# Pooled attention, mixture of experts and a cosine FFN on one core: a written-out order of steps for each attention unit in place of one order for all

## The chip, the cores and the metric

One core of a Trainium2 chip runs the whole program in one launch. The metric is the device time of an execution in microseconds; the time before is the median of three runs. The profile comes from one further execution, taken by the hardware profiler. PE is TensorE, DVE VectorE, ACT ScalarE, POOL GpSimd and SP SyncE; each engine works off its own queue in order.

## The reference

The output of the attention is the input of the mixture of experts (MoE), and its output that of the last FFN. Cut to what is computed:

```python
# attention: q, k, v (8, 8, 576, 64)
k_p = k.reshape(B, H, Sp, pool, D).mean(axis=3)      # pool = 8, Sp = 72
v_p = v.reshape(B, H, Sp, pool, D).mean(axis=3)
scores = scale * np.matmul(q, k_p.transpose(0, 1, 3, 2))
attn = softmax(scores)
x = np.matmul(attn, v_p)                             # as (4608, 512)
# MoE: 8 experts, the 2 best by noisy logits, w1 (8, 512, 1024), w2 (8, 1024, 512)
noisy_logits = x @ w_gate + np.log1p(np.exp(x @ w_noise)) * noise
out[mask] += top2_w[mask, k, None] * (np.maximum(x[mask] @ w1[e], 0.0) @ w2[e])
# last FFN, d_ff = 2048
h = x @ w_in
return (h * np.cos(h)) @ w_out
```

## The kernel before, in words

**Stages.** The program runs three stages after one another: attention with the gating of the MoE and the scatter of its rows (0 to about 335 us of the profiled execution), the experts, and the last FFN. The change touches the code of the first stage alone.

**Pairs and units.** The eight batches are worked in four pairs (`g` = 0 to 3). A pair has nine row blocks of 64 positions of both batches, 128 rows; two row blocks make a unit, and the fifth unit of a pair has one. That makes 20 units (`UNITS`), numbered 0 to 19; units 4, 9, 14 and 19 are the small ones.

**Steps of a unit.** The loop over `u` (line 747 on) issues the steps of several units interleaved: 
- `S0` to `S3` are `scores(u+2)`: matmuls of q with the pooled K (L432) and DVE's maximum (L434);
- `E0` to `E3` are `expo(u+2)`: ACT's exponentials (L447);
- `N` is `soft_sum(u+1)`: DVE's sum and reciprocal (L457 to L461), and then the multiply of the exponentials by it (L462), on POOL for all units but the last;
- `T0` to `T2` are `e_tr(u)`: PE transposes of the exponentials (L479 to L483) into a PSUM buffer `tr`, of which there are two, and ACT's copy out of it (L485);
- `A0` to `A3` are `av(u)`: matmuls with V (L513), ACT's copy to `xr` (L516), DVE's remainder (L517) and logits (L520, L522);
- `Q0`, `Q1` are `q_tr(u+3)`: transposes of q (L416) and ACT's copy (L417);
- `G` issues steps of the fill list.

Only the order of issue is chosen here: every engine takes its instructions in the order in which the loop issues them, and waits where an operand or a buffer isn't ready.

**The fill list.** It holds work that isn't of the running unit, as a list of functions. For the next pair (`setup_steps`): five steps that pool K (by DVE, or for pairs 2 and 3 by `folded`, with matmuls by the identity, L298), five that pool V, four transposes of K (L313, ACT L320), `scale_v`, four transposes of V (L313), two steps of the projection of the gate's weights (`g_proj1`, `g_proj2`, L372 and L384). For the pair before (`late`): the gating in ten steps (`gating`, L526 on; g1 to g6 below, with `g1` from L546 on, `g3` L559 to L562, `g4a` and `g4b` L569 to L577, `g5` the matmuls of L583 to L588, `g5b` the indices `idx` at L605) and nine `scatter` steps. One `scatter` (L634) has two indirect DMAs (L639) that POOL issues, each behind a one-element memset (L638). In pairs 2 and 3 the list also holds the preparation of the first expert's weights (`prep_steps`): for each weight four `amax` reductions on DVE (L153), of which the last ends with the copy `mbc` (L108), a `scl` step that begins with a PE transpose of `mbc` (L114), and eight steps that split the weights (ACT L171 and DVE L178). In units 18 and 19 it holds four `up` steps (`early_up`, twelve matmuls each, L662) and four `lo` steps.

**What sets the order before.** One string is used for all units (line 738):

```python
ORDER = "S0 G T0 G T1 S1 E0 T2 N A0 G A1 E1 S2 G A2 Q0 E2 G S3 G A3 Q1 G E3".split()
```

At each of its seven `G`, `go` issues the next steps of the list, their number so chosen that the list is spread evenly over what is left of the pair. At a pair border two lists are merged evenly by `mix`.

Of the kernel before, what the change touches and what calls it, by code (L numbers as in the profile page):

```python
# [12 lines left out]
AF = mybir.ActivationFunctionType  # L13
# [12 lines left out]
T0 = [E * 1024 + 128 * i + sum(EXTRA[:i]) for i in range(E)]  # L26
# [11 lines left out]
def tile_attn_moe_ffn(ctx: ExitStack, tc: tile.TileContext, q, k, v, wgate, wnoise, noise,  # L38
                      w1, w2, win, wout, out):
    nc = tc.nc  # L40
    V, A, PL, PE, SP = nc.vector, nc.scalar, nc.gpsimd, nc.tensor, nc.sync

    def dap(src, offset, dims):
        return bass.AP(tensor=src.tensor, offset=src.offset + offset, ap=dims)
# [22 lines left out]
    idf = const.tile([128, 128], F32, name="idf")  # L67
    V.tensor_scalar(idf, jp, 0.0, None, op0=OP.is_equal)

    QT, KT, VT = {}, {}, {}  # L70

    def nop():
        pass

    def load_kv(g, which):
        src, dst = ((k, KT), (v, VT))[which]
        t = ow.tile([128, 5, 2, 512], F32, name="w1", bufs=2)
        for c in range(5):
# [186 lines left out]
    def setup_steps(g):  # L265

        X = {}
        kbd = KBDB[g % 2]

        def pooled(src, nm, i):  # L270
            def f():
                if i == 0:
                    X[nm + "f"] = src.pop(g).rearrange("p c b e -> p (c b) e")
                    n0, n1 = (0, 1280) if nm == "ks" else (1280, 1920)
                    X[nm] = SW[:, n0:n1].rearrange("p (c s d) -> p c s d", c=10, d=D)
                t, o = X[nm + "f"], X[nm]
                n = 64 if nm == "ks" and i == 4 else 128
                t, o = t[0:n, 2 * i:2 * i + 2, :], o[0:n, 2 * i:2 * i + 2, :, :]
                for w in (256, 128):
                    V.tensor_add(t[:, :, 0:w], t[:, :, 0:w], t[:, :, w:2 * w])  # L280
                dup = [n, 2, 2 if nm == "ks" else 1, D]
                V.tensor_add(o, t[:, :, None, 0:D].to_broadcast(dup), t[:, :, None, D:2 * D].to_broadcast(dup))
            return f

        def folded(src, nm, i):

            def f():
                if i == 0:
                    X[nm + "f"] = src.pop(g).rearrange("p c b e -> p (c b) e")
                    n0, n1 = (0, 1280) if nm == "ks" else (1280, 1920)  # L290
                    X[nm] = SW[:, n0:n1].rearrange("p (c s d) -> p c s d", c=10, d=D)
                if i in (0, 4):
                    X["pf"] = pq.tile([128, 512], F32, name="sc", bufs=3)
                t = X["pf"]
                c0, c1, js = (0, 8, range(2 * i, 2 * i + 2)) if i < 4 else (8, 10, range(8))
                n = 64 if nm == "ks" and i == 4 else 128
                for j in js:
                    PE.matmul(t[0:n, 0:64 * (c1 - c0)].rearrange("p (c d) -> p c d", d=D), idf[0:n, 0:n],  # L298
                              X[nm + "f"][0:n, c0:c1, 64 * j:64 * j + 64], start=(j == 0), stop=(j == 7))
                if js[-1] == 7:  # L300
                    k_ = 2 if nm == "ks" else 1
                    A.activation(X[nm][0:n, c0:c1], t[0:n, 0:64 * (c1 - c0)].rearrange("p (c d) -> p c d", d=D)[:, :, None, :]
                                 .to_broadcast([n, c1 - c0, k_, D]), AF.Copy)
            return f

        def tr_half(src, b, half):
# [84 lines left out]

        bh = [(b, h) for b in range(2) for h in range(2)]
        pk, pv = ([pooled(src, nm, i) for i in range(5)] for src, nm in ((KT, "ks"), (VT, "vp")))
        if g in (2, 3):
            pk = [folded(KT, "ks", i) for i in range(5)]
        if g in ():
            pv = [folded(VT, "vp", i) for i in range(5)]
        kt, vt = ([f(*x) for x in bh] for f in (k_tr, v_tr))
        return pk, kt, pv, [scale_v, nop, scale_v2] + vt + [g_proj1, nop, g_proj2]

# [5 lines left out]
    def q_tr(u, half):  # L406
        if u >= NU:
            return
        g, r, n = UNITS[u]
        qt = QT[g]  # L410
        if half == 0:
            QTS[u] = ap_.tile([128, 8, 128], F32, name="qs", bufs=2)
        qs, h0 = QTS[u], 4 * half
        tr = pq.tile([128, 512], F32, name="tr", bufs=2)
        for h in range(4):
            PE.transpose(tr[0:64 * n, 128 * h:128 * h + 128], qt[:, h0 + h, 64 * r:64 * (r + n)], idf)  # L416
        A.activation(qs[0:64 * n, h0:h0 + 4, :], tr[0:64 * n].rearrange("p (h t) -> p h t", h=4), AF.Copy)  # L417
# [316 lines left out]
    fill, late = [], []  # L734

    CUTS = {3: (0, 6), 4: (6, 8)}
    left = [0]
    ORDER = "S0 G T0 G T1 S1 E0 T2 N A0 G A1 E1 S2 G A2 Q0 E2 G S3 G A3 Q1 G E3".split()

    def go():  # L740
        k_ = -(-len(fill) // left[0])
        left[0] = max(left[0] - 1, 1)
        for f in fill[:k_]:
            f()
        del fill[:k_]

    for u in range(NU):
        g, r, n = UNITS[u]
        it = u % 5
        if it == 0:  # L750
            a = []
            if g + 1 < G:
                pk, kt_, pv, sv = setup_steps(g + 1)
                a = pk + pv[:2]
                for i in range(4):
                    a += kt_[i:i + 1] + pv[i + 2:i + 3]
                a += sv
                if g + 2 < G:
                    a.append(lambda g=g: (load_kv(g + 2, 0), load_kv(g + 2, 1)))
            if g == G - 1:  # L760
                a = p2
            fill += mix(a, late)
            late = []
        if g == G - 2 and it == 2:
            p1, p2 = prep_steps(0, "w1"), prep_steps(0, "w2")
            p1.pop(0)()
            p2.pop(0)()
        if g == G - 2 and it == 3:
            fill = mix(fill, p1)
        if g == G - 1 and it in CUTS:  # L770
            r0, r1 = CUTS[it]
            gt = gating(g, r0, r1)
            gt.pop(0)()
            fill += with_ups(gt, (0, 1) if it == 3 else (2, 3)) + [scatter(g, r_) for r_ in range(r0, r1)]
        left[0] = ORDER.count("G") * ((5 if g < G - 1 or it > 2 else 3) - it)
        if g == G - 1 and it == 3:
            left[0] = 6
        for op in ORDER:
            k_ = int(op[1:] or 0)
            if op == "A0":  # L780

                while first_v:
                    first_v.pop(0)()
            if op[0] == "G":
                go()
            elif op[0] == "S":
                scores(u + 2, k_)
            elif op[0] == "E":
                expo(u + 2, k_)
            elif op[0] == "N":  # L790
                soft_sum(u + 1)
            elif op[0] == "T":
                e_tr(u, k_)
            elif op[0] == "A":
                av(u, k_ // 2, k_ % 2)
            else:
                q_tr(u + 3, k_)
# [86 lines left out]
    with tc.For_i(0, nov, 1) as i:  # L884
# [496 lines left out]
    o = work.index((mm2, JOBS.index((E - 1, 0)), 3))  # L1381
# [80 lines left out]
    for c in range(NCF):  # L1462
        plan = prepare(c + 1, lambda: g[:, 14:16, :])
        for q_ in range(4):
# [4 lines left out]
            g = GQ[c, q_] = wp.tile([128, 16, 512], F16, name="ht", bufs=2)  # L1469
# [82 lines left out]
```

## Time and profile before

| | us |
|---|---|
| median of 3 runs | 1796.01 |
| lowest, highest | 1793.70, 1797.31 |
| profiled execution, whole | 1813.74 |
| its span | 1811.6 |
| PE busy in the span | 1733.1 (96%) |
| DVE, ACT, POOL busy | 1052.0, 923.9, 425.0 |
| mean granted clock of PE | 0.976 |
| PE idle after 335 us | 11.45 of 1476.00 |

The page gives the busy time of each engine and the span in 40 slices; the view by stretches gives the same for any piece of the span, with PE's granted clock in it (1.00 is full speed). A timeline lists one engine's instructions in order, with the idle time before each and what ended it in brackets: `[1.35 <-ACT et L485]` is 1.35 us of waiting that ACT's write of `et` at line 485 ended. Neighbouring instructions of one form stand in one row with their count (x3).

### The profile page before, as it was taken

The page shows a single profiled execution, that of the slowest core. Times are in us where ns is not written, and L with a number is a line of the kernel's source. Part 1 is how long each engine was busy: PE and PEld are TensorE (multiplying, and loading weights), DVE is VectorE, ACT ScalarE, POOL GpSimd, SP SyncE. Part 2 cuts the span into 40 slices and gives each one's busy share as a digit, 9 for nine tenths or more (in the row PEclk, how much of TensorE's full clock was granted, in tenths as well). Part 3 has the DMA queues.
Part 4 walks back from the last instruction along what each step waited for, and adds up shares of the span by engine and source line. Part 5 has one row for each costly group of instructions (what it writes and reads, how often), then busy time and mean ns, then how long its engine had stood idle before and what let it go on. Part 6 is the DMA issues. An engine that isn't in the chain of part 4 may idle for free.

```text
span 1811.6 us, 28368 instructions
## 1 busy us (share of the span) xinstructions
PE 1733.1 (96%) x11105; PEld 1014.1 (56%) x11105; DVE 1052.0 (58%) x2010; ACT 923.9 (51%) x1836; POOL 425.0 (23%) x459
## 2 busy tenths in 40 slices
PE   5999787899999999999999998999999999999999
PEld 3665553355444644454545545666666666666665
DVE  7675674464567376435766135665656566565633
ACT  4776563132333233222323225777777777767765
POOL 1225536100001000001110013424334343333222
PEclk8999868999999999999999999999999999999999
DMA  9987524558453836464572734313223031322200
GB/s 269 309 282 273 209 60 163 155 163 230 125 177 111 243 106 194 151 184 138 140 233 88 261 94 128 88 40 72 70 66 83 29 88 53 76 58 61 42 24 24
DMA packets 231144, 242.57 MB, mean 134 GB/s; under 512 B 152513, under 2 KB 165825, under 8 KB 230369
## 3 DMA queue, kind: packets, MB, share of 16 engines
q1 hardware_dynamic: 208752, 183.51, 35.7%
q0 software_dynamic: 11520, 37.76, 6.6%
q10 hardware_dynamic: 10736, 19.47, 3.0%
q8 instruction: 88, 1.44, 0.3%
q14 instruction: 48, 0.39, 0.1%
HBM read 127.06 MB, written 77.66 MB: 113 GB/s over the span
## 4 chain that ended last, share of the span: by engine, by line
PE 77%; DVE 3%; ACT 1%; issue 0%; ACTq 0%; DVEq 0%
PE ph L1445 20%; PE py L972 20%; PE ph L662 19%; PE py L1408 15%; PE pt L1408 3%; PE py L987 1%; DVE w L178 0%; DVE amw L153 0%; DVE ty L1420 0%; DVE ht L960 0%; DVE ty L1064 0%; DVE ty L1066 0%; DVE ty L1065 0%; ACT ty L1112 0%; DVE ty L1113 0%
## 5 line engine op out<-in xcount | busy, mean ns | idle before, releaser
L1445 PE MATMUL ph<-sw,ht 128*128 128x512 f16 x1152 | 383.6, 380 | 0.0
L662 PE MATMUL ph<-xt,w 128*128 128x512 f16 (+3 forms) x2208 | 377.5, 329 | 0.2 <-DVE ht L960 0.2
L662 PEld LDWEIGHTS <-w 128*128 128x128 f16 x2304 | 207.5, 99 | 190.9 <-issue 11.5
L1435 POOL TENSOR_TENSOR ht<-ty,ht 128x512 f16<-128x512 f32 x144 | 183.8, 1282 | 473.3 <-ACT ht L1434 365.3
L972 PEld LDWEIGHTS <-ht 128*128 128x128 f16 (+1 forms) x1656 | 161.0, 98 | 191.5 <-DVE ht L960 1.5
L960 DVE SCALAR_TENSOR_TENSOR ht<-ph,ht 128x512 f16<-128x512 f32 (+3 forms) x184 | 102.1, 561 | 273.4 <-ACT ht L959 266.1
L1445 PEld LDWEIGHTS <-ht 128*128 128x128 f16 x1728 | 169.5, 98 | 152.3 <-issue 0.8
L1445 PE MATMUL ph<-w,ht 128*128 128x512 f16 x576 | 218.8, 380 | 0.0
L1408 PEld LDWEIGHTS <-st 128*128 128x128 f16 x1872 | 183.2, 98 | 54.6 <-issue 3.7
L972 PE MATMUL py<-w,ht 128*128 128x512 f16 x864 | 192.2, 379 | 1.1 <-ACT ht L959 0.7
L959 ACT ACTIVATE ht<-ph 128x512 f16<-128x512 f32 (+3 forms) x184 | 89.8, 492 | 173.2 <-PE ph L662 158.8
L972 PE MATMUL py<-sw,ht 128*128 128x512 f16 (+1 forms) x792 | 176.5, 379 | 0.1
L975 ACT ACTIVATE yt<-py,ysc 128x512 f32<-128x512 f32 x73 | 50.1, 686 | 242.2 <-PE py L972 237.6
L1408 PE MATMUL py<-xt,st 128*128 128x256 f16 x1040 | 139.3, 273 | 3.3 <-ACT ht L1498 3.3
L1420 DVE SCALAR_TENSOR_TENSOR ty<-ty,k,ht 128x512 f32<-128x512 f32 x108 | 94.1, 871 | 81.7 <-ACT ty L1414 80.8
L1429 DVE SCALAR_TENSOR_TENSOR ty<-ty,ht 128x512 f32<-128x512 f32 x108 | 74.8, 692 | 108.7 <-ACT ty L1426 104.8
L1408 PEld LDWEIGHTS <-w 128*128 128x128 f16 x1152 | 112.9, 98 | 39.5 <-issue 4.3
L1425 ACT ACTIVATE ty<-ty,k 128x512 f32<-128x512 f32 x144 | 102.8, 714 | 21.8 <-DVE ty L1420 21.7
L1408 PE MATMUL py<-w,st 128*128 128x256 f16 x832 | 111.7, 273 | 0.0
L1414 ACT ACTIVATE ty<-ht,k 128x512 f32<-128x512 f32 x108 | 77.4, 717 | 67.3 <-DVE ht L1481 33.2
L1434 ACT ACTIVATE ht<-ty 128x512 f16<-128x512 f32 x144 | 89.5, 621 | 34.9 <-DVE ty L1429 34.3
L1056 POOL TENSOR_TENSOR tm<-yg 128x512 f32<-128x512 f32 x32 | 33.8, 1055 | 293.5 <-DVE x L1066 183.6
(287 smaller groups left out, 2336.8 us busy)
## 6 DMA issues: line engine op xcount, KB each, us to landing
yb<-yt ACTq DMA_DIRECT2D x72, 256.0 KB
yg<-in_moe_w_in_dram SPq DMA_DIRECT2D x32, 512.0 KB
yg<-in_moe_w_out_dram SPq DMA_DIRECT2D x32, 512.0 KB
st<-in_moe_w_dram SPq DMA_DIRECT2D x7, 2048.0 KB
yb<-zt SPq DMA_DIRECT2D x18, 768.0 KB
st<-in_moe_w_dram SPq DMA_DIRECT2D x8, 1536.0 KB
w<-in_k_dram SPq DMA_DIRECT2D x16, 512.0 KB
w<-in_v_dram SPq DMA_DIRECT2D x16, 512.0 KB
```

The lines of the kernel that those rows point to most:

```text
L662: PE.matmul(ps[:, 0:n], w[:, a_, k_, 128 * f:128 * f + 128], xt[:, 4 * b_ + k_, 0:n], start=(i == 0), stop=(i == 11))
L959: A.activation(t[:, 0], p, AF.Relu)
L960: V.scalar_tensor_tensor(t[:, 1], p, 0.0, t[:, 0], op0=OP.max, op1=OP.subtract)
L972: PE.matmul(ps[0:m], ht[:, a_, f, 128 * t:128 * t + m], w[:, b_, f, :], start=(i == 0), stop=(i == 23))
L1408: PE.matmul(o, FW["in"][4 * a_ + 2 * sa + k_][:, f:f + 128], x[:, :, sb, k_, :], start=(start and h == 0 and k_ == 0 and j == 0), stop=(k_ ...
L1414: A.activation(y, h, AF.Identity, bias=CB["k4", c][:, 0:1])
L1420: V.scalar_tensor_tensor(y, y, CB["k4", c][:, 0:1], h, op0=OP.subtract, op1=OP.subtract)
L1425: A.activation(y, y, AF.Sin, scale=CB["k4", c][:, 1:2])
L1429: V.scalar_tensor_tensor(UB[b][3], UB[b][3], CC, UB[b][2], op0=OP.subtract, op1=OP.mult)
L1434: A.activation(g[:, 2 * b, :], y, AF.Copy)
L1435: PL.tensor_sub(g[:, 2 * b + 1, :], y, g[:, 2 * b, :])
L1445: PE.matmul(ps, g[:, 2 * b + a_, 256 * h + 128 * tt:256 * h + 128 * tt + 128], FW["out"][b_][:, k_, :], start=(q_ == 0 and b < 2 and h == ...
```

## The change

`ORDER` and `go` are replaced by `PLAN`, a string for each of the 20 units, in which `Gk` issues the next k steps of the fill list. `mix` at the pair borders is replaced by `merge` with `MIX`, a string for each border, in which a letter names the list from which the next step comes (K and k the pooling and the transposes of K, V and s the pooling of V and the rest of its setup, L the load, l the pair before, w the weights, f what is left of the fill list, n nothing). `folded` takes a number `m` of slices per step from a table `FOLD`, in place of the fixed two. The diff, cut to its core (of the tables two rows):

```diff
+    FOLD = {"k": (0, 0, 2, 2), "v": (0, 0, 0, 0)}
...
-        def folded(src, nm, i):
+        def folded(src, nm, i, m):
...
-                if i in (0, 4):
+                if i in (0, 8 // m):
...
-                c0, c1, js = (0, 8, range(2 * i, 2 * i + 2)) if i < 4 else (8, 10, range(8))
-                n = 64 if nm == "ks" and i == 4 else 128
+                c0, c1, js = (0, 8, range(m * i, m * i + m)) if i < 8 // m else (8, 10, range(8))
+                n = 64 if nm == "ks" and c0 else 128
...
-        if g in (2, 3):
-            pk = [folded(KT, "ks", i) for i in range(5)]
+        if FOLD["k"][g]:
+            pk = [folded(KT, "ks", i, FOLD["k"][g]) for i in range(8 // FOLD["k"][g] + 1)]
...
-    ORDER = "S0 G T0 G T1 S1 E0 T2 N A0 G A1 E1 S2 G A2 Q0 E2 G S3 G A3 Q1 G E3".split()
-
-    def go():
-        k_ = -(-len(fill) // left[0])
-        left[0] = max(left[0] - 1, 1)
-        for f in fill[:k_]:
-            f()
-        del fill[:k_]
+    PLAN = [
...
+        "S0 G1 T0 E0 S1 T1 T2 N A0 S2 A1 E1 A2 G1 Q0 E2 A3 G2 S3 Q1 E3 G2",
...
+    MIX = [
...
+        "fwfwfwwfffwwfwffwwwffwfnwfnwff"]
+
+    def merge(how, **lists):
+        lists = {c: list(x) for c, x in lists.items()}
+        out = [nop if c == "n" else lists[c].pop(0) for c in how]
+        assert not any(lists.values())
+        return out
...
-            fill += mix(a, late)
+                fill += merge(MIX[g], K=pk, k=kt_, V=pv, s=sv, L=ld, l=late)
+            else:
+                fill += merge(MIX[g], w=p2, l=late)
...
-            fill = mix(fill, p1)
+            fill = merge(MIX[G], f=fill, w=p1)
...
-        left[0] = ORDER.count("G") * ((5 if g < G - 1 or it > 2 else 3) - it)
-        if g == G - 1 and it == 3:
-            left[0] = 6
-        for op in ORDER:
+        for op in PLAN[u].split():
...
-                go()
+                for f in fill[:k_]:
+                    f()
+                del fill[:k_]
```

What moves, at three places. On PE in unit 13, from S2 to the transpose of `mbc` (L114, in the changed kernel L115), which begins the scale step of w1; L432 are scores, L313 the transposes of V, L513 the step A2, L416 the step Q0. Before:

```order
L432 MATMUL sc<-kbd_110,qs 64x2x72 x4
L313 MATMUL sc<-idf,sw 64x128 x2
L313 MATMUL sc<-idf,sw 64x64
L513 MATMUL xp<-vbd,et 64x144 x2
L513 MATMUL xp<-vbd,et 64x208 x2
L513 MATMUL xp<-vbd,et 64x64 x2
L416 MATMUL tr<-idf,st 128x128 x4
L114 MATMUL tr<-idf,mbc 128x128
```

Now:

```order
L432 MATMUL sc<-kbd_110,qs 64x2x72 x4
L313 MATMUL sc<-idf,sw 64x128 x2
L313 MATMUL sc<-idf,sw 64x64
L313 MATMUL sc<-idf,sw 64x128 x3
L513 MATMUL xp<-vbd,et 64x144 x2
L513 MATMUL xp<-vbd,et 64x208 x2
L513 MATMUL xp<-vbd,et 64x64 x2
L416 MATMUL tr<-idf,st 128x128 x4
L432 MATMUL sc<-kbd_110,qs 64x2x72 x4
L115 MATMUL tr<-idf,mbc 128x128
```

A second transpose of V and the step S3 now stand ahead of the transpose of `mbc`; the last `amax` step, which stood between the first transpose of V and A2, now stands ahead of A1.

On POOL between the multiplies for units 17 and 18 (L462; `xr` and its number is the row block that a scatter sends; of the five row blocks before, two are shown). Before:

```order
L462 TENSOR_TENSOR ex_2900<-ex_2900,rc_3108 128x1152
L638 MEMSET spacer_103 1x1
L639 DMA xs_62<-xr_2111,idx_64 38400x1024
L638 MEMSET spacer_103 1x1
L639 DMA xs_62<-xr_2111,idx_64 38400x1024
L638 MEMSET spacer_103 1x1
L639 DMA xs_62<-xr_2258,idx_64 38400x1024
L638 MEMSET spacer_103 1x1
L639 DMA xs_62<-xr_2258,idx_64 38400x1024
...
L639 DMA xs_62<-xr_2470,idx_64 38400x1024
L462 TENSOR_TENSOR ex_3095<-ex_3095,rc_3263 128x1152
```

Now, whole:

```order
L462 TENSOR_TENSOR ex_2898<-ex_2898,rc_3102 128x1152
L638 MEMSET spacer_103 1x1
L639 DMA xs_62<-xr_2278,idx_64 38400x1024
L638 MEMSET spacer_103 1x1
L639 DMA xs_62<-xr_2278,idx_64 38400x1024
L638 MEMSET spacer_103 1x1
L639 DMA xs_62<-xr_2310,idx_64 38400x1024
L638 MEMSET spacer_103 1x1
L639 DMA xs_62<-xr_2310,idx_64 38400x1024
L462 TENSOR_TENSOR ex_3087<-ex_3087,rc_3255 128x1152
```

Ten issues stood between the two multiplies, and now four do. Ahead of the first of the two multiplies stood the two issues of one scatter since the indices came, and now the four of two.

On PE in unit 19, from T0 on: L479 and L481 are transposes of the exponentials, L513 is A0, L662 an `up` step. Before:

```order
L479 MATMUL tr<-idf,ex 128x128 x4
L481 MATMUL tr<-idf,ex 64x128
L513 MATMUL xp<-vbd,et 64x144 x2
L513 MATMUL xp<-vbd,et 64x208 x2
L513 MATMUL xp<-vbd,et 64x64 x2
```

Now (the pair of L662 rows stands there twelve times):

```order
L479 MATMUL tr<-idf,ex 128x128 x3
L662 LDWEIGHTS w_2685
L662 MATMUL sc<-kbd_108,w_2685 128x512
...
L479 MATMUL tr<-idf,ex 128x128
L481 MATMUL tr<-idf,ex 64x128
L513 MATMUL xp<-vbd,et 64x144 x2
L513 MATMUL xp<-vbd,et 64x208 x2
L513 MATMUL xp<-vbd,et 64x64 x2
```

The `up` step that followed A0 now stands between T0 and T1. In unit 12 the last transpose of K moves from behind S0 to ahead of it; in unit 15 `g3` moves from behind N's neighbours T0 and A0 to ahead of T0 and N, `g4a` stands behind A0, and `g5b` and `g6`, which stood in unit 16 behind S0 and T0, stand in unit 15 behind A3 and Q1. On POOL the multiply for unit 14 stands behind two more issues than before.

## Rows read from the trace of the kernel before

**Rows 1.** The page: PE's granted clock in 40 slices of the span, in tenths.
```profile
PEclk8999868999999999999999999999999999999999
```

**Rows 2.** Stretches: us from:to and length, busy us (instructions) PE PEld DVE ACT POOL, PE clock, DMA share, GB/s.
```profile
60.00:120.00 60.00, 58.96 (x576) 40.29 (x576) 41.44 (x123) 44.77 (x169) 13.03 (x12) 1.00 1.04 345
120.00:194.00 74.00, 66.09 (x652) 44.64 (x648) 51.35 (x158) 50.40 (x184) 34.29 (x49) 1.00 0.61 213
194.00:202.00 8.00, 8.00 (x64) 5.59 (x62) 3.88 (x11) 4.20 (x17) 3.33 (x4) 0.57 1.04 312
225.00:245.00 20.00, 18.72 (x105) 12.32 (x107) 11.41 (x22) 14.10 (x50) 7.35 (x9) 0.50 0.38 106
335.00:1811.00 1476.00, 1464.55 (x8833) 839.90 (x8831) 830.13 (x1341) 736.63 (x1180) 290.90 (x250) 1.00 0.41 115
```

**Rows 3.** Timeline of PE, units 12 to 14: start, us, instruction [idle before <-releaser].
```profile
193.68 0.33 PE L479 MATMUL tr<-idf,ex 128*128 128x128 f32 x1 [1.35 <-ACT et L485]
...
210.12 0.58 PE L313 MATMUL sc<-idf,sw 128*64 128x128 f32 x3
210.63 0.93 PE L513 MATMUL xp<-vbd,et 128*64 128x144 f32 x12
211.49 0.66 PE L416 MATMUL tr<-idf,st 128*128 128x128 f32 x4
214.66 0.42 PE L114 MATMUL tr<-idf,mbc 128*128 128x128 f32 x1 [2.51 <-DVE mbc L108]
...
219.12 0.71 PE L432 MATMUL sc<-kbd,qs 128*64 128x144 f32 x8
...
226.28 1.66 PE L513 MATMUL xp<-vbd,et 128*64 128x144 f32 x12 [1.91 <-ACT et L485]
```

**Rows 4.** Timeline of ACT, unit 12: a fill step's eviction ahead of the unit's own.
```profile
192.28 0.82 ACT L320 ACTIVATE kbd<-sc 64x288 f32<-64x288 f32 x2
```

**Rows 5.** Timelines of POOL, DVE and PE in unit 15, apart.
```profile
246.50 2.11 POOL L462 TENSOR_TENSOR ex<-ex,rc 128x1152 f32<-128x1152 f32 x1 [9.09 <-ACT xr L516]
...
246.83 1.86 DVE L559 TENSOR_TENSOR g_lu<-g_lu,g_u 128x72 f32<-128x72 f32 x1
248.73 0.23 DVE L560 TENSOR_TENSOR g_lu<-g_lu,nz 128x72 f32<-128x72 f32 x1
...
254.50 1.21 DVE L153 TENSOR_REDUCE amw<-w 128x1 f32<-128x1024 f32 x1
...
256.31 0.44 PE L114 MATMUL tr<-idf,mbc 128*128 128x128 f32 x1 [6.90 <-DVE mbc L108]
```

**Rows 6.** Timeline of POOL: multiplies for units 17 and 18, scatter issues.
```profile
262.74 1.87 POOL L639 DMA_INDIRECT xs<-xr,idx  x1 [14.10 <-DVE idx L605]
...
267.05 2.11 POOL L462 TENSOR_TENSOR ex<-ex,rc 128x1152 f32<-128x1152 f32 x1 [1.17 <-DVE rc L461]
...
280.85 0.96 POOL L639 DMA_INDIRECT xs<-xr,idx  x1 [0.21 <-issue]
...
282.12 0.98 POOL L639 DMA_INDIRECT xs<-xr,idx  x1 [0.21 <-issue]
283.12 2.13 POOL L462 TENSOR_TENSOR ex<-ex,rc 128x1152 f32<-128x1152 f32 x1
```

**Rows 7.** Timeline of PE: T0 of unit 17, the end of unit 17, T0 of unit 18.
```profile
270.69 0.55 PE L479 MATMUL tr<-idf,ex 128*128 128x128 f32 x3
...
273.93 3.56 PE L513 MATMUL xp<-vbd,et 128*64 128x144 f32 x48
285.30 0.90 PE L479 MATMUL tr<-idf,ex 128*128 128x128 f32 x3 [7.81 <-POOL spacer L638]
```

**Rows 8.** Timeline of PE: unit 19 and the end of the stage.
```profile
302.25 0.93 PE L513 MATMUL xp<-vbd,et 128*64 128x144 f32 x12 [3.25 <-ACT et L485]
...
328.22 2.75 PE L662 MATMUL sc<-kbd,w 128*128 128x512 f16 x12
334.73 1.89 PE L972 MATMUL py<-sw,st 128*128 128x512 f16 x4 [3.76 <-DVEq L884]
```

More of the change, by code (lines that the diff above doesn't have):

```diff
@@ L291, in f @@
                     X[nm] = SW[:, n0:n1].rearrange("p (c s d) -> p c s d", c=10, d=D)
-                if i in (0, 4):
+                if i in (0, 8 // m):
                     X["pf"] = pq.tile([128, 512], F32, name="sc", bufs=3)
                 t = X["pf"]
-                c0, c1, js = (0, 8, range(2 * i, 2 * i + 2)) if i < 4 else (8, 10, range(8))
-                n = 64 if nm == "ks" and i == 4 else 128
+                c0, c1, js = (0, 8, range(m * i, m * i + m)) if i < 8 // m else (8, 10, range(8))
+                n = 64 if nm == "ks" and c0 else 128
+                o = t[0:n, 0:64 * (c1 - c0)].rearrange("p (c d) -> p c d", d=D)
                 for j in js:
-                    PE.matmul(t[0:n, 0:64 * (c1 - c0)].rearrange("p (c d) -> p c d", d=D), idf[0:n, 0:n],
-                              X[nm + "f"][0:n, c0:c1, 64 * j:64 * j + 64], start=(j == 0), stop=(j == 7))
+                    PE.matmul(o, idf[0:n, 0:n], X[nm + "f"][0:n, c0:c1, 64 * j:64 * j + 64], start=(j == 0), stop=(j == 7))
                 if js[-1] == 7:
-                    k_ = 2 if nm == "ks" else 1
-                    A.activation(X[nm][0:n, c0:c1], t[0:n, 0:64 * (c1 - c0)].rearrange("p (c d) -> p c d", d=D)[:, :, None, :]
-                                 .to_broadcast([n, c1 - c0, k_, D]), AF.Copy)
+                    A.activation(X[nm][0:n, c0:c1], o[:, :, None, :].to_broadcast([n, c1 - c0, 2 if nm == "ks" else 1, D]),
+                                 AF.Copy)
             return f
@@ L393, in setup_steps @@
         pk, pv = ([pooled(src, nm, i) for i in range(5)] for src, nm in ((KT, "ks"), (VT, "vp")))
-        if g in (2, 3):
-            pk = [folded(KT, "ks", i) for i in range(5)]
-        if g in ():
-            pv = [folded(VT, "vp", i) for i in range(5)]
+        if FOLD["k"][g]:
+            pk = [folded(KT, "ks", i, FOLD["k"][g]) for i in range(8 // FOLD["k"][g] + 1)]
+        if FOLD["v"][g]:
+            pv = [folded(VT, "vp", i, FOLD["v"][g]) for i in range(8 // FOLD["v"][g] + 1)]
         kt, vt = ([f(*x) for x in bh] for f in (k_tr, v_tr))
@@ L736, in tile_attn_moe_ffn @@
     CUTS = {3: (0, 6), 4: (6, 8)}
-    left = [0]
-    ORDER = "S0 G T0 G T1 S1 E0 T2 N A0 G A1 E1 S2 G A2 Q0 E2 G S3 G A3 Q1 G E3".split()
-    def go():
-        k_ = -(-len(fill) // left[0])
-        left[0] = max(left[0] - 1, 1)
-        for f in fill[:k_]:
-            f()
-        del fill[:k_]
+    PLAN = [
[20 rows of a table added]
+    MIX = [
+        "KKKVKKVkVkVVkkssssssssssL",
+        "lKKlKllKlKVlVkVlkVllklVnklssllsslslslslsslLls",
+        "KllKlKKlKlVllVllVklVklVklklslslsslllsssllslnssl",
+        "lwllwwllwlwlwllwllwllwlwwllwwlll",
+        "fwfwfwwfffwwfwffwwwffwfnwfnwff"]
[4 more added lines that the diff above has]
+        return out
     for u in range(NU):
@@ L750, in tile_attn_moe_ffn @@
         if it == 0:
-            a = []
             if g + 1 < G:
                 pk, kt_, pv, sv = setup_steps(g + 1)
[L754 to L761, printed above, removed]
-            fill += mix(a, late)
+                ld = [lambda g=g: (load_kv(g + 2, 0), load_kv(g + 2, 1))] if g + 2 < G else []
+                fill += merge(MIX[g], K=pk, k=kt_, V=pv, s=sv, L=ld, l=late)
+            else:
+                fill += merge(MIX[g], w=p2, l=late)
             late = []
```

19 rows, old and new, of the table PLAN are left out of this document.

## The prediction

> **What bounds the kernel now.** I read the page's slices first: the granted clock of TensorE (PE) is under nine tenths only in the first and the fifth to seventh of 40 slices, so before 317 us [rows 1]. The next view is the table by stretches, to see where PE idles. From 335 us to the end PE is busy 1464.55 of 1476.00 us; the change doesn't touch that stage, which starts when the attention stage lets it. From 60 to 120 us PE is busy 58.96 of 60.00 us: units 0 to 6 have hardly a gap to close. From 120 to 194 us some 8 us are idle, in pieces of about 1 us at full clock. Between 194 and 335 us it is different: gaps, and stretches behind them at a granted clock of 0.50 to 0.57, the lower of PE's two levels, 1.2 in place of 2.4 GHz [rows 2]. So the change can be worth something where PE waits after 190 us, and each of those waits has a named releaser in the PE timeline [rows 3, 5, 7, 8]. PE bounds this stage; a wait of PE that goes is time gained one for one.
>
> The sum is made against the profiled execution: 1813.74 us, of which 1811.6 are its span. The median of the runs shown is 1796.01, so 17.7 us less. Since the stage after 335 us has 11 us of idle PE in all, most of that difference must lie in the attention stage; some of the losses below may be of the profiled execution alone. I take from the median only what the order of the queues causes, and keep the rest for the range.
>
> **The change part by part.** No instruction goes or comes; matmuls, evictions, reductions and DMAs are the same in number and size, and SP's queue keeps its order. `folded` and `FOLD` give the same five steps of K for pairs 2 and 3 as before. These parts cost nothing. What moves are steps of the fill list against the steps of a unit on PE, ACT, DVE and POOL.
>
> *Unit 12, T1.* PE waits 1.35 us [rows 3] because ACT evicts the K transpose of the fill step before the unit's own transposes (0.82 us for the two [rows 4]). Now that fill step is issued ahead of S0 and T0, so PE has S0 and T0 to do while ACT evicts. Gain 1.35, bounds 0 and 1.35.
>
> *Unit 13, the scale of w1.* The PE step waits 2.51 us for DVE's `mbc` [rows 3]. Between the last `amax` step and the scale step PE had only A2 and Q0: 0.93+0.66 = 1.59 us, so the chain takes 1.59+2.51 = 4.10 us. Now A1, S2, two V transposes, A2, Q0 and S3 lie between: 0.93+0.71+0.58+0.58+0.93+0.66+0.71 = 5.10 us [rows 3], more than 4.10. Gain 2.51. DVE has the reductions of S2 and S3 and two more evictions in that time too, so the lower bound is 1.
>
> *Unit 15, the scale of w2.* The largest wait but one, 6.90 us [rows 5], does not go: the last 1.21 us reduction ends at 255.71 and PE starts at 256.31 [rows 5], so DVE's own queue is the chain: gating steps, four such reductions and the evictions of this unit, which are all still ahead of the scale step. What goes is one piece. L559 took 1.86 us where L560, of the same shape, took 0.23; it ends when the multiply on POOL ends (246.83+1.86 = 248.69, 246.50+2.11 = 248.61 [rows 5]). Now L559 is issued with g3, ahead of N, whose reciprocal releases the multiply. Gain 1.86-0.23 = 1.63, which DVE hands to PE in full.
> The Trainium skill has a rule for this, SBUF — State Buffer, "Who interferes with whom": a VectorE operation with two SBUF inputs and a GpSimd operation that reads SBUF share a port pair, and whichever issues first holds it for its whole instruction. The pair of rows agrees. The rule speaks against the change here, since g4a, with two-input operations of its own, now follows N: if one of them meets the multiply, this gain is 0 and the sum below falls by 1.6 us.
> By the rows the bounds are 0, if an operation of g4a is held up as L559 was, and 1.63. I take 1.63, because w2's 1.21 us reduction [rows 5] and the evictions of A0 stand between N and g4a and cover most of the multiply's 2.11 us.
>
> *Unit 18, T0.* This is the largest wait, 7.81 us [rows 7]. The unit's transposes need POOL's multiply, which stood behind 12 scatter issues: the first starts at 262.74, when `idx` is there, and the multiply ends at 283.12+2.13 = 285.25, 22.5 us later [rows 6]. POOL issues in order, and one issue with its spacer takes 1.27 us (280.85 to 282.12 [rows 6]). Now 8 issues and two multiplies lie there: 8 x 1.27 + 2.11+2.13 = 14.4 us; if two issues are as slow as the first (1.87 in place of 0.96) and POOL waits for `rc` again (1.17), 17.4 [rows 6]. PE reached T0 at 273.93+3.56 = 277.49 [rows 7], 14.75 us behind the first issue. `idx` now comes earlier against PE's work, because g5b and g6 stand before S3 and Q1 of unit 15 and S0 of unit 16 are all done: 0.71+0.66+0.71 = 2.1 us more of PE work lie between. So PE arrives at 16.8, POOL is ready at 14.4 to 17.4. Gain 7.81, lower bound 7.2.
> The cover is then gone for what follows: gating of the last pair's first six blocks (g1 to g4b) stands ahead of PE's `g5`. I charge 1 us of new wait, between 0 and 2.
>
> *Unit 19, A0.* PE waits 3.25 us for the evictions of the unit's transposes [rows 8]. Now the twelve matmuls of `up2`, 2.75 us for as many at full clock [rows 8], stand between T0 and T1, while ACT and DVE run the gating that held the eviction. Gain 2.75, bounds 0 and 3.25. The 3.76 us before the next stage [rows 8] stay.
>
> The sum: 1.35+2.51+1.63+7.81+2.75-1 = 15.05 us. 1796.0-15 = **1781 us**.
>
> Not in the sum: a wait in unit 14 of 1.91 us [rows 3], where the order changes too, and the slow clock itself. In 225 to 245 us PE is busy 18.72 us at 0.50; at full clock that is half, 9.4 us less. In 194 to 202 us it is 8.00 us at 0.57, 3.4 us less [rows 2]. Both stretches begin behind a wait (1.35 us at 193.68; 1.91 at 226.28 [rows 3]), while the stretches behind shorter gaps before 190 us show full clock [rows 2]. If all that goes, it is 1.9+9.4+3.4 = 15 us more, some 1766. I keep this for the low end only, since the median is 17.7 us below the profiled execution and may have had part of it already.
>
> **The rivals.** *The tail is POOL's* (12%). After unit 18's multiply POOL now has 22 scatter issues without a multiply in between, 28 us. If the last PE steps hang on these, or on evictions that come late beside them, nothing gained in units 18 and 19 reaches the end but the 2.1 us by which `idx` is earlier: 1.35+2.51+1.63+2.1 = 7.6 us, **1788**. For it: POOL issues almost without a pause between 262.74 and 285.25 [rows 6]. Against: 22 issues from about 276 us end before 305, and PE has work until 328.22+2.75 = 331 [rows 8].
>
> *Nothing that shows* (15%). The waits are DVE's and ACT's total work in disguise: a wait removed at one step comes back at the next, as in unit 15. Then only unit 18's T0 gains part of its 7.81, and under 3.6 us is left: **1794**. A measurement of this kernel can tell about 0.2%, 3.6 us, from no change. For it: in unit 15 PE's wait is for DVE's `mbc`, which stands behind DVE's other work [rows 5]; against: in units 12, 18 and 19 the releaser is a place in a queue.
>
> *Slower* (13%). The multiplies for units 14 and 17 each stand behind two more scatter issues, 2 x 1.27 = 2.54 us. For unit 17 the multiply ended at 267.05+2.11 = 269.16 [rows 6] and T0 began at 270.69 [rows 7]: 1.5 us of slack, so it decides from there. If both become PE waits of 2.5 us, and each is followed by a stretch like 225 to 245 us (9.4 us lost [rows 2]), that is 2 x 11.9 = 24 us against the 15: **1805**. For it: such stretches do follow waits of 1.4 us and more. Against: unit 17's T0 also gets POOL's first issues earlier against PE, by the 2.1 us above, and of unit 14's T0 no wait for POOL is seen now.
>
> **How the numbers follow.** The forecast has 60%; its own range is 1766 to 1790 (the lower bounds of the terms give 0+1+0+7.2+0-2 = 6 us, 1790). The range of 8 in 10 takes in the tail and the case of no change up to their upper ends: 1766 to 1799; it leaves out the slower case and what might lie below the low end. Faster by over 0.2%: the forecast and the tail, 60+12 = 72%; within 0.2%: 15%; slower: 13%.
>
> **What would show it.** Right: no PE wait for POOL at T0 of unit 18, the waits of 1.35, 2.51 and 3.25 us gone, and about 5.3 us left of the 6.90 in unit 15; PE starts the next stage some 15 us earlier, in stretches with fewer slices under full clock. Wrong: new PE waits for POOL's multiply at T0 of units 14 or 17, or scatters that end after PE's last attention step (tail), or the same idle sum in 190 to 335 us with other releasers (no change). If the idle sum falls and the time doesn't, the loss was the profiled execution's own.

## The result, and the profile after

The change takes 1774.8 us (median of 4, 1772.85 to 1776.2) against 1795.8 us before: 21.0 us less, ratio 0.988 with a 95% interval of 0.987 to 0.990. The forecast was 1781, range 1766 to 1799. Timed on two later occasions, the gain is smaller, 12.6 and 9.9 us (e5 and e10 below), on both beside a time before of about 1820 us; that difference is a finding of its own here. The profiled execution of the change took 1772.85 us, near its median; that of before, on which the working rests, lay 17.7 us above its median, so the 40 us between the two spans are not the size of the change. Its 1813.74 us lie outside the 1793.7 to 1797.3 us of the runs beside it and inside the 1811.2 to 1826.4 us that before took on the later occasions. So the rows on which the forecast rests look like those of the later occasions.

The page of the change, the lines that answer to [rows 1]:

```profile
PE 1710.2 (97%) x11105; PEld 1003.5 (57%) x11105; DVE 1043.2 (59%) x2010; ACT 921.4 (52%) x1836; POOL 424.4 (24%) x459
...
PEclk8999999999999999999999999999999999999999
```

Instructions are the same in number; PE's clock is under nine tenths in the first slice only. The view by stretches (columns as in [rows 2]):

```profile
187.00:212.00 25.00, 23.41 (x253) 16.25 (x254) 20.93 (x59) 20.21 (x71) 19.10 (x33) 1.00 0.93 337
212.00:234.00 22.00, 12.76 (x123) 8.68 (x121) 18.11 (x49) 13.13 (x49) 12.48 (x16) 0.91 0.45 137
234.00:254.00 20.00, 18.90 (x216) 12.82 (x212) 15.18 (x43) 16.60 (x58) 14.37 (x18) 0.93 0.28 106
254.00:294.20 40.20, 29.60 (x199) 15.29 (x199) 30.37 (x143) 12.92 (x32) 29.20 (x55) 0.96 0.48 185
294.20:1770.00 1475.80, 1463.62 (x8833) 839.50 (x8833) 829.19 (x1341) 736.34 (x1180) 290.96 (x250) 1.00 0.41 115
```

The last row is the stage behind attention: 1475.8 us with 1463.6 busy, as before (1476.0 and 1464.6). The whole difference lies ahead of it, which now ends at 294.2 in place of 334.7 us. The stretch at a clock of 0.50 for 20 us [rows 2] has no counterpart. PE's timeline, units 12 to 19, at the places of [rows 3, 5, 7, 8]:

```profile
186.55 0.33 PE L479 MATMUL tr<-idf,ex 128*128 128x128 f32 x1 [0.19 <-DVE g_gap L627]
203.74 0.33 PE L115 MATMUL tr<-idf,mbc 128*128 128x128 f32 x1
207.25 0.66 PE L479 MATMUL tr<-idf,ex 128*128 128x128 f32 x4 [0.53 <-POOL spacer L638]
213.86 0.66 PE L372 MATMUL tr<-sw,wgn 64*16 64x144 f32 x4 [1.27 <-ACT sw L374]
231.93 0.44 PE L115 MATMUL tr<-idf,mbc 128*128 128x128 f32 x1 [7.07 <-DVE mbc L109]
254.01 0.55 PE L479 MATMUL tr<-idf,ex 128*128 128x128 f32 x3
265.44 0.55 PE L479 MATMUL tr<-idf,ex 128*128 128x128 f32 x3
270.03 1.82 PE L513 MATMUL xp<-vbd,et 128*64 128x144 f32 x24 [1.24 <-ACT et L485]
294.26 12.43 PE L989 MATMUL py<-sw,st 128*128 128x512 f16 x48 [5.74 <-issue]
```

In the order of the forecast: unit 12's wait is 0.19 in place of 1.35; unit 13's scale step (L115) doesn't wait, where it waited 2.51; a new wait of 0.53 for POOL stands at T0 of unit 14, the place that the rival "slower" named; unit 15 still waits, 7.07; T0 of unit 18 (254.01) has no wait, where it was 7.81; unit 19 waits 1.24 in place of 3.25; the experts begin behind a wait of 5.74 in place of 3.76. In unit 14 the wait of 1.91, which the sum left out, is gone, and one of 1.27 stands at L372. POOL and DVE at the multiplies (two timelines):

```profile
225.09 2.11 POOL L462 TENSOR_TENSOR ex<-ex,rc 128x1152 f32<-128x1152 f32 x1 [1.47 <-DVE rc L461]
236.69 1.01 POOL L639 DMA_INDIRECT xs<-xr,idx  x1 [9.45 <-DVE ohcb L608]
251.84 2.11 POOL L462 TENSOR_TENSOR ex<-ex,rc 128x1152 f32<-128x1152 f32 x1 [1.24 <-DVE rc L461]
...
221.50 0.22 DVE L559 TENSOR_TENSOR g_lu<-g_lu,g_u 128x72 f32<-128x72 f32 x1
226.60 0.69 DVE L570 TENSOR_TENSOR g_tmp<-g_lv,g_m 128x72 f32<-128x72 f32 x1
```

The multiply for unit 18 ends 17.3 us behind the first issue (251.84+2.11-236.69; 14.4 to 17.4 had been worked out), just ahead of T0. L559 takes 0.22. L570, now the first operation of DVE with two SBUF inputs behind the multiply that unit 15 issues (for unit 16), is held until the multiply ends: 226.60+0.69 = 227.29 against 225.09+2.11 = 227.20. That is the rule of the Trainium skill that was weighed (SBUF — State Buffer, "Who interferes with whom"); in this case it took back 0.5 us of the 1.6.

### The profile page after: what moved, and what is told of

It reads as the page before. It is cut to its first block, busy times and chain, and to the rows that moved or that the text cites. A ratio compares the mean times of both kernels' runs of the same rounds, so it can differ in the third digit from the quotient of the medians.

```text
span 1771.0 us, 28368 instructions
## 1 busy us (share of the span) xinstructions
PE 1710.2 (97%) x11105; PEld 1003.5 (57%) x11105; DVE 1043.2 (59%) x2010; ACT 921.4 (52%) x1836; POOL 424.4 (24%) x459
## 4 chain that ended last, share of the span: by engine, by line
PE 86%; DVE 7%; ACT 3%; POOL 1%; issue 1%; DMA 0%; ACTq 0%; POOLq 0%; DVEq 0%
PE ph L1462 21%; PE py L989 20%; PE ph L662 19%; PE py L1425 15%; PE pt L1425 3%; PE xp L513 2%; PE sc L432 2%; PE sc L300 1%; DVE w L281 1%; POOL xs L639 1%; ACT ex L447 1%; PE tr L416 1%; PE tr L479 1%; DVE amw L154 1%; PE py L1004 1%
## 5 line engine op out<-in xcount | busy, mean ns | idle before, releaser
L662 PE MATMUL ph<-xt,w 128*128 128x512 f16 (+3 forms) x2208 | 377.5, 329 | 0.2 <-DVE ht L977 0.2
L662 PEld LDWEIGHTS <-w 128*128 128x128 f16 x2304 | 205.7, 98 | 184.5 <-issue 1.6
## 6 DMA issues: line engine op xcount, KB each, us to landing
yb<-zt SPq DMA_DIRECT2D x18, 768.0 KB, 17.3
w<-in_v_dram SPq DMA_DIRECT2D x16, 512.0 KB, 12.6
```

The costliest lines, as they stand in the source:

```text
L662: PE.matmul(ps[:, 0:n], w[:, a_, k_, 128 * f:128 * f + 128], xt[:, 4 * b_ + k_, 0:n], start=(i == 0), stop=(i == 11))
```

## The experiments

The order of before can be written in the tables of the change. So each experiment is an edit of `PLAN` and `MIX`. Two theories were tested: A, the waits that the order of the queues causes add up to the gain; B, the half clock behind waits makes the larger part.

**e1 to e4: by pairs.** The tables mixed by pair; e1 has all of them of before.

```diff
# e3: PLAN rows 10 to 14, MIX[2] and MIX[4] of the change, the others as before; row 15:
-        "S0 G3 S1 G2 T0 E0 T1 T2 N A0 G2 A1 E1 G2 S2 A2 Q0 E2 G2 A3 G4 S3 Q1 G2 E3",
+        "S0 G2 T0 G2 T1 S1 E0 T2 N A0 G2 A1 E1 S2 G2 A2 Q0 E2 G2 S3 G2 A3 Q1 G2 E3",
```

e1. 

> The order of before, written in the tables of the change: every engine's queue is the same as before, so every theory expects the time of before, ratio 1.000 within 0.002. Its profile tells what belongs to one profiled execution: theory A (losses caused by the order of the queues) expects the PE waits of 1.35, 2.51, 6.90, 7.81 and 3.25 us again, each within 0.5 us, and, if the slow stretches follow from those waits, also 225 to 245 us at a clock near 0.5 and a span near 1811. Theory C (the slow stretches are that one execution's own) expects the waits again but fewer slow stretches and a span near 1794.

e2. 

> The new order in pairs 0 and 1 alone (units 0 to 9), the old one in units 10 to 19. Theory A expects no gain: 0 to 2 us, since PE had no gaps in units 0 to 6. Rival: the profiled times at N of unit 10 are 4 us earlier with the whole change, so if these are kept to the end, 4 us faster, 1791 to 1792.

e3. 

> The new order in pair 2 alone (units 10 to 14). Theory A, waits alone: 1.35 + 2.51 = 3.9 us, 1792. Theory B (a wait costs also the slow clock behind it): the stretches of 194 to 202 and 225 to 245 us go too, up to 12.8 us more, so 1780 to 1785.

e4. 

> The new order in pair 3 alone (units 15 to 19). Theory A: 1.63 + 7.81 + 2.75 - 1 = 11.2 us, 1784 to 1785. Theory B: the slow stretches of 252 to 263 and 278 to 290 us behind the waits of 6.90 and 7.81 us go too, 2 to 5 us more, 1780. If a gain in pair 3 needs pair 2's new order, under 6 us.

The time before was 1819.1 us here. Ratios and intervals: e1 1.001 (0.9995 to 1.003), e2 1.001 (1.000 to 1.003), e3 0.997 (0.995 to 0.998), e4 0.998 (0.996 to 1.000); by medians +2.6, +2.3, -6.7 and -3.9 us. Pairs 0 and 1 bring nothing, as forecast: beside e1's profile, POOL's multiplies in e2's run 3.6 us ahead at 104 us, level at 121 and 5.4 ahead at 156, and then 2.9 behind at 176, so the lead is not kept. Pair 2 gains 3 to 9 us by its interval, which holds A's 3.9 and ends short of B's 11 to 16. Pair 3 stays well under A's 11.2, and its interval reaches to no gain at all. e1's profile shows the waits of before again (1.35, 2.54, 7.79 and, in unit 19, 3.37 us); that of unit 15 is 8.18 in place of 6.90, so outside the 0.5 us that had been expected. Its span of 1817.6 us is near its own median. So the waits belong to the order, and beside a time of 1820 us stretches at half clock come with them.

**e5: the change again.** 

> The change itself, beside the order of before on the same chip. The parts alone gave 0 (pairs 0 and 1), -6.2 us (pair 2) and -3.5 us (pair 3), sum -10. Theory A (waits add up): ratio 0.994 to 0.995. Theory B (the slow clock behind waits joins neighbouring parts, so that the parts gain more together than alone): ratio about 0.988, as when the change was first timed, 21 us.

1807.9 against 1820.5 us, ratio 0.993 (0.992 to 0.995). The parts add up: 0-6.7-3.9 = -10.6 against -12.6, on another chip. No gain from joining them shows beyond the noise, and the ratio of 0.988 that B expects lies outside the interval, so B's "more together than alone" is not borne out here. But the same program ends its attention stage at 328.4 us here and at 294.3 us in its first profile. The stretches and PE's timeline of e5 show where:

```profile
150.00:163.00 13.00, 10.23 (x72) 6.48 (x66) 3.67 (x10) 6.61 (x26) 7.76 (x12) 0.61 1.04 409
...
223.00:257.00 34.00, 25.15 (x202) 17.24 (x202) 27.48 (x71) 20.83 (x70) 14.36 (x18) 0.70 0.31 94
...
291.00:328.00 37.00, 25.50 (x121) 11.17 (x121) 21.84 (x110) 8.12 (x21) 18.81 (x35) 0.82 0.34 129
```

```profile
275.64 0.55 PE L479 MATMUL tr<-idf,ex 128*128 128x128 f32 x3
...
286.30 0.34 PE L513 MATMUL xp<-vbd,et 128*64 128x208 f32 x1 [0.21 <-issue]
287.02 0.39 PE L513 MATMUL xp<-vbd,et 128*64 128x208 f32 x1 [0.38 <-issue]
...
292.73 0.90 PE L479 MATMUL tr<-idf,ex 128*128 128x128 f32 x3
...
304.01 0.38 PE L662 MATMUL sc<-kbd,w 128*128 128x512 f16 x1 [1.04 <-issue]
306.12 1.32 PE L662 MATMUL sc<-kbd,w 128*128 128x512 f16 x2 [1.74 <-issue]
308.95 5.82 PE L662 MATMUL sc<-kbd,w 128*128 128x512 f16 x20 [1.51 <-issue]
```

Matmuls that follow each other without a gap elsewhere come singly here, 0.7, 1.4 or 2.1 us apart, with no releaser. ACT and POOL at that time (two timelines):

```profile
289.97 0.66 ACT L516 ACTIVATE xr<-xp 128x256 f16<-128x256 f32 x2 [6.60 <-remote]
...
308.26 0.38 ACT L516 ACTIVATE xr<-xp 128x256 f16<-128x256 f32 x1 [10.53 <-remote]
...
275.47 1.01 POOL L639 DMA_INDIRECT xs<-xr,idx  x1 [0.15 <-issue]
...
287.25 0.96 POOL L639 DMA_INDIRECT xs<-xr,idx  x1 [0.21 <-issue]
291.83 0.96 POOL L639 DMA_INDIRECT xs<-xr,idx  x1 [3.53 <-DVE idx L605]
...
305.78 0.96 POOL L639 DMA_INDIRECT xs<-xr,idx  x1 [0.21 <-issue]
```

PE slows some 11 us after a burst of scatter issues begins (275.47 to 286.30; from 291.83 on, it had slowed by 304.01) and recovers 2 to 3 us after the burst's last issue has ended. In the same time ACT reads PE's results late: it waits 6.60 and 10.53 us for A steps. This is theory C: bursts of issues slow PE and its reports. PE did not wait for its instructions there: no transfer of the queues that carry instructions runs between 278.3 and 298.4 us in this trace. Unit 18, T0 to T0 of unit 19, takes 17.1 us here and 11.4 us in the first profile of the change (265.44-254.01), where POOL issues just as densely (without a pause from 254 to 289 us) and none of this is seen. So a burst alone is not enough.

**e6 and e7: two parts undone.**

```diff
# e6, unit 17: two scatters ahead of N, so of the multiply for unit 18
-        "S0 G1 T0 E0 S1 T1 T2 N A0 S2 A1 E1 A2 G1 Q0 E2 A3 G2 S3 Q1 E3 G2",
+        "S0 G1 T0 E0 S1 T1 T2 G2 N A0 S2 A1 E1 A2 Q0 E2 A3 G1 S3 Q1 E3 G2",
# e7, unit 13: the scale step of w1 behind S2 (MIX[4] to match)
-        "S0 G3 T0 G3 T1 S1 E0 N T2 A0 G2 A1 E1 S2 G2 A2 Q0 E2 S3 G3 A3 Q1 E3",
+        "S0 G3 T0 G3 T1 S1 E0 N T2 A0 G2 A1 E1 S2 G1 A2 Q0 E2 S3 G4 A3 Q1 E3",
```

e6. 

> The change, but with two more scatters (four issues, 4 x 1.27 = 5.1 us) ahead of POOL's multiply for unit 18. In the profile of the change PE reaches T0 of unit 18 when that multiply ends, with nothing to spare. Theory A: a PE wait of 4 to 5 us for POOL there, and 4 to 5 us slower than the change. Theory B: a slow stretch behind the wait too, 6 to 10 us slower. Rival D (the end of the stage is set by something else, so that the 7.81 us were not the path): under 1.5 us slower.

e7. 

> The change, but in unit 13 the scale step of w1 stands behind S2 again, with A1 and S2 (1.6 us) behind the last amax step. Theory A: the PE wait of about 2.5 us for mbc is back and the time is 2.5 us longer. Theory B: the stretch behind it runs at a clock of 0.5 to 0.6, 3 to 9 us longer. Rival (the wait is absorbed by unit 15's wait for DVE, whose work does not start later): under 1 us.

e6: 1807.5 us, ratio 0.993 (0.991 to 0.995), no slower than e5. PE reaches T0 of unit 18 at 281.24, 5.6 us later than in e5, and T0 of unit 19 at 292.96, only 0.2 us later:

```profile
281.24 0.90 PE L479 MATMUL tr<-idf,ex 128*128 128x128 f32 x3
...
289.47 3.56 PE L513 MATMUL xp<-vbd,et 128*64 128x144 f32 x48
292.96 0.55 PE L479 MATMUL tr<-idf,ex 128*128 128x128 f32 x3
```

The expected wait for POOL is not there: PE itself arrives 2.3 us behind the multiply's end (278.94), held up in unit 17, where POOL's eight issues now stand in one row and PE is at half clock from 272 to 282 us; how much of the delay each makes isn't shown. In return, with six issues behind the multiply instead of ten, the A steps of unit 18 run at one stretch (3.56 us). So rival D's number holds for another reason: in these two profiles the issues cost about the same ahead of the multiply and behind it. What the earlier multiply wins in the change is paid back within the unit.

e7: 1810.7 us, ratio 0.995 (0.993 to 0.997), by medians 2.8 us slower than e5; the intervals overlap, so 2.8 isn't told from 0 with certainty. The wait is back (2.24). Half clock adds up to less than in e5 (41 against 51 us after 60 us), but e7's profile is of an execution 4.2 us below its median (1806.48 us), so this does not settle B, and 2.8 us lie between A's 2.5 and the low end of B:

```profile
215.58 0.45 PE L115 MATMUL tr<-idf,mbc 128*128 128x128 f32 x1 [2.24 <-DVE mbc L109]
```

**e8: w2 taken out of unit 15.**

```diff
-            fill = merge(MIX[G], f=fill, w=p1)
+            fill = merge(MIX[G], f=fill, w=p1, z=[p2.pop(0), p2.pop(0)])
# units 15 and 16 (rows 14 and 17, MIX[3] and MIX[4] follow):
-        "S0 G3 S1 G2 T0 E0 T1 T2 N A0 G2 A1 E1 G2 S2 A2 Q0 E2 G2 A3 G4 S3 Q1 G2 E3",
-        "S0 G1 T0 G2 E0 S1 N T1 T2 A0 G2 A1 E1 S2 Q0 A2 E2 G1 A3 Q1 S3 G1 E3",
+        "S0 G2 S1 G2 T0 E0 T1 T2 N A0 G1 A1 E1 G2 S2 A2 Q0 E2 G1 A3 S3 Q1 E3",
+        "S0 G4 T0 G2 E0 S1 N T1 G1 T2 A0 G2 A1 E1 S2 G1 Q0 A2 E2 G1 A3 Q1 S3 G2 E3",
```

> The change, but with two of the four 1.21 us reductions of w2 moved from unit 15 to unit 14, and the scale of w2 and the gating's matmuls moved behind A3, S3, Q1 of unit 15 and S0 of unit 16; scatters moved behind the multiply for unit 17, three of them ahead of that for unit 18. Theory A: the PE wait of 7.07 us falls to 1 to 3 us, 4 to 6 us faster than the change. Theory B: the clock behind it stays at 1, 6 to 9 us faster. Rival (DVE's total work sets units 14 to 16): the wait comes back in units 14 or 16, under 2 us.

1811.5 us, ratio 0.996 (0.994 to 0.998): slower than e5 by 3.7 by medians, and the intervals overlap. The profile is of an execution 9.4 us above that median, 1820.93 us. The wait falls from e5's 6.48 to 2.04 and comes back at the next step of the chain, 3.15 for the gating, as the rival said. The scatters, which now start later, end later. They also stand in one row of 24, from 278.67 to 310.02 us, and PE's matmuls come singly until 313.1, with gaps of up to 2.2 us, so for longer behind a longer row, as theory C has it.

```profile
252.37 0.30 PE L115 MATMUL tr<-idf,mbc 128*128 128x128 f32 x1 [2.04 <-DVE g_m L569]
255.82 0.22 PE L583 MATMUL tr<-g_ohb,lt 128*128 128x72 bf16 x1 [3.15 <-DVE lg L522]
...
297.58 0.68 PE L479 MATMUL tr<-idf,ex 128*128 128x128 f32 x2 [1.04 <-issue]
...
307.48 0.59 PE L662 MATMUL sc<-kbd,w 128*128 128x512 f16 x1 [2.23 <-issue]
...
311.67 0.59 PE L662 MATMUL sc<-kbd,w 128*128 128x512 f16 x1 [2.21 <-issue]
```

**e9 and e10: before and the change on a third occasion.** The kernels of e1 and e5 again.

e9. 

> The order of before once more, to stand beside the change on one chip with a profile of each. If the size of the gain belongs to the occasion (the change gained 21 us when the median of before was 1796, and 12.6 us when it was 1820), then a median near 1796 here goes with few stretches at half clock before 190 us, and one near 1820 with stretches at half clock from 150 us on.

e10. 

> The change once more. Beside a before of about 1820: ratio 0.991 to 0.995, PE matmuls that come singly with gaps put down to no releaser behind bursts of scatter issues, and half clock for 45 to 55 us after 60 us. Beside a before of about 1796: ratio 0.987 to 0.990, none of these, and half clock for under 25 us after 60 us.

e9 takes 1817.9 us beside a before of 1818.2, and e10 1808.3, ratio 0.994 (0.992 to 0.996). Slow stretches begin at 154 us in e9 and at 149 us in e10. Summed over the trace's clock records, PE is at half clock for 48 us after 60 us in e10 and for 17 us in the first profile of the change. Single matmuls are there in both (e9 from 309 us on). The later occasions were on three chips (e1 to e4, e5 to e8, e9 to e12), and before took about 1820 us on each; on which chip it took 1796 isn't known, so the chip may be what differs.

**e11: the burst behind the multiply taken away.**

```diff
-                fill += merge(MIX[g], w=p2, l=late)
+                hold = late[-5:]
+                fill += merge(MIX[g], w=p2, l=late[:-5])
...
+            fill += hold if it == 4 else []
# PLAN rows 17 to 19 and MIX[3] follow
```

> The change, but the last five scatters of pair 2 (ten issues) moved behind all steps of unit 19, so that POOL issues nothing between its multiply for unit 18 and the gating indices of the last pair. Theory C (bursts of scatter issues delay PE's steps and their reports): the single matmuls and late evictions that e5 shows at 284 to 291 us, in unit 18, are gone, and PE reaches the last up step 3 to 6 us earlier. Rival (they follow PE's own queue or the slow clock): they stay. The whole time may be up to 5 us longer than the change's all the same, since the last rows land 13 us later behind the last issue.

```profile
279.32 0.55 PE L479 MATMUL tr<-idf,ex 128*128 128x128 f32 x3 [0.71 <-POOL spacer L638]
...
286.50 3.56 PE L513 MATMUL xp<-vbd,et 128*64 128x144 f32 x48
...
289.99 0.55 PE L479 MATMUL tr<-idf,ex 128*128 128x128 f32 x3
...
336.25 2.31 PE L991 MATMUL py<-sw,st 128*128 128x512 f16 x5 [14.31 <-DVEq L903]
```

The first four lines are e11's; e10's unit 18, T0 to T0:

```profile
271.65 0.55 PE L479 MATMUL tr<-idf,ex 128*128 128x128 f32 x3 [0.71 <-POOL spacer L638]
...
288.56 0.90 PE L479 MATMUL tr<-idf,ex 128*128 128x128 f32 x3
```

Unit 18 takes 10.7 us (289.99-279.32), 6.2 less than in e10 (16.9), and neither single matmuls nor late evictions are left in it: theory C holds for this unit. e4, e7 and e12, which keep the ten issues there, take 17.3, 16.1 and 17.4 us. The slow clock is not the reason: e5's single matmuls of unit 18 (286 to 291 us) fall between two stretches at half clock (271 to 274 and 291 to 295). Whether POOL's issuing or the transfers it starts do it isn't told apart, since e11 moves both. Behind the next row, in unit 19, the single matmuls are there in e11 as well. The last gating matmul comes 36.0 us behind T0 of unit 18, and 41.8 in e10, so 5.8 less, as expected (3 to 6); it isn't earlier counted from the start, since e11's profile, of an execution 3.9 us above its median (1816.93 us), reaches unit 18 7.7 us later.

The whole is 1813.1 us, ratio 0.997 (0.995 to 0.999), by medians 4.8 above e10, for another reason: PE waits 14.31 us ahead of the experts, 10.5 more than in e10. Less the 5.8, that is 4.7. The moved issues end later, and the experts wait for POOL's last one. In all these profiles the experts begin 7.7 to 8.1 us behind the start of POOL's last issue, and 5.9 in the first profile of the change:

| | last issue | last gating matmul | experts begin |
|---|---|---|---|
| before | 326.68 | 323.84 | 334.73 |
| change, first | 288.33 | 281.80 | 294.26 |
| e5 | 320.31 | 317.47 | 328.38 |
| e6 | 321.09 | 318.25 | 328.83 |
| e10 | 316.32 | 313.48 | 324.06 |
| e11 | 328.57 | 315.32 | 336.25 |
| e12 | 318.89 | 316.05 | 326.63 |

In most rows the last issue itself follows the last gating matmul by 2.84 us, and that matmul stands 10.6 to 10.9 us ahead of the experts: both bounds come from the same step. In e11, and by some 2 us (294.26-281.80 = 12.5) in the first profile of the change, POOL was still busy with the row ahead, and its issues alone decide.

**e12: unit 15's wait covered.**

```diff
-        "S0 G3 S1 G2 T0 E0 T1 T2 N A0 G2 A1 E1 G2 S2 A2 Q0 E2 G2 A3 G4 S3 Q1 G2 E3",
+        "S0 G3 S1 G2 T0 E0 T1 T2 N A0 G2 A1 E1 G2 S2 A2 Q0 E2 A3 S3 Q1 G2 E3 G6",
```

> The change, but in unit 15 the steps A3, S3 and Q1 stand ahead of the scale step of w2 and of the gating's matmuls; nothing else is moved. Theory A: these 2.3 us of PE work come out of the 7.07 us wait, 2 to 3 us faster than the change, wait 4 to 5 us. Rival (what is gained there is lost again before the end of the stage, as the four more issues ahead of the multiply for unit 18 cost nothing in e6): within 1.5 us of the change, though the wait is shorter.

```profile
251.20 0.45 PE L115 MATMUL tr<-idf,mbc 128*128 128x128 f32 x1 [4.17 <-DVE mbc L109]
253.22 0.22 PE L583 MATMUL tr<-g_ohb,lt 128*128 128x72 bf16 x1 [1.58 <-ACT qs L417]
```

The wait falls to the 4 to 5 us expected, from 5.80 in e10 on the same occasion, and 1.58 come back at the next step. The time is 1807.0 us, ratio 0.994 (0.992 to 0.996), against e10's 1808.3: within 1.5 us, as the rival said. A gain over the change isn't shown.

## Why the prediction was right, and where it wasn't

The time, the direction and the order of size were right: 15 us forecast, 21 measured, 10 to 13 on the later occasions. That the sum lies between them is in part luck, since several terms missed. By steps:

- *Units 12 and 13.* Right; both waits are gone (0.19 us is left of the first), and undoing the second brings back 2.24 of the 2.51 us. Its price in time, 2.8 us by medians, is in line with the term but not told from 0.
- *Unit 15.* "About 5.3 us left of the 6.90" was wrong: 7.07 are left. DVE's stretch from the first of w2's reductions to `mbc` did shrink, from 15.1 to 12.2 us, and L559 with it, but PE now comes to the step earlier as well. A wait for a busy engine is no measure of what a cut in that engine's work gives. e12 then cut this wait by 1.6 us against e10, for no measurable gain.
- *Unit 18.* The wait went as worked out, and POOL's 17.3 us lay in the range worked out. That it is "gained one for one" failed on the later occasions. There, ten issues behind the multiply slow the unit by 5 to 6 us (e5 and e10 against e6 and e11). 15.05 less 5.5 is 9.6 us, and 9.9 and 12.6 were measured; the agreement is no proof, since without the terms that units 15 and 19 missed it would be 7.2. The row is also longer than worked out: 28 issues follow the multiply, not 22. The rival "the tail is POOL's" had named the mechanism, evictions that come late beside the row of issues, and gave 7.6.
- *The 1 us of new wait in unit 18.* Right in place and size: 0.59 us at `g5` in the first profile of the change.
- *Unit 19 and the end.* 1.24 are left, so 2.0 gained, not 2.75. "The 3.76 us before the next stage stay" holds on the later occasions, but in the first profile 5.74 stand there: POOL's row of issues ends last, which costs the 2 us seen above. This too is what the rival "the tail is POOL's" had named.
- *The slow clock*, kept for the low end: in the first profile of the change it is mostly gone, and the 6 us above the sum fit that. By the upper bounds of the terms alone, 16.6 us, the range would have ended at 1779, so it is this low end that holds the 1774.8. That the clock made the 6 us is argued: no profile of before at 1796 us exists, so how much half clock that execution had isn't known.
- *The rivals.* "Nothing that shows" and "slower" did not come; of the slower case's waits, 0.53 us at unit 14 is all in the first profile.

Open: why the same program shows the bursts' effect on two occasions and not on the first, which moves the time before by 23 us and that of the change by 33; the chip is a rival that no run rules out. An estimate for the change: 51 us at half clock in e5 against 17 in its first profile make up to (51-17)/2 = 17 us, and unit 18 alone takes 5.7 us more. A kernel without the scatters would tell whether their traffic is the cause; it wasn't tried, since it would read memory that nothing has written.

## What to carry to other kernels

When a step moves from ahead of a wait to behind it, ask what it does to the work that it now runs beside: a row of DMA issues that no longer delays a multiply may slow the matmuls behind it by nearly as much. Read a stage's end by all queues that its successor waits for: here it is the last PE gating step and POOL's last issue, so a gain in the middle of the stage counts only if both come earlier. Time a scheduling change on more than one occasion before giving its size.

## What was not expected of the hardware

Some 11 us into a dense row of POOL's scatter issues (one per 1.27 us) PE's matmuls came singly, 0.7 to 2.1 us apart, and ACT waited 6.60 and 10.53 us for PE's results, until 2 to 3 us after the row's end; in e8, with a row of 24 issues, they still came singly at its end, 31 us on. The six issues behind the multiply in e6 did not do this, nor did any row in the first profile of the change. The end of the same program's attention stage lay at 294 us and at 328 us on two occasions.
